# An order table, a head-by-head start and VectorE adds in a fused attention and feed-forward kernel

## The chip, the cores and the metric

The kernel runs on one core of a Trainium2 chip. The metric is device time in microseconds; of the kernel before, three runs were taken: 113.99, 114.84 and 115.63, median 114.84. PE is TensorE, DVE is VectorE, ACT is ScalarE, POOL is GpSimd, SP is SyncE, which only issues transfers here.

## What is computed

Attention with a polynomial sketch (batch 4, 4 heads, 1088 tokens, head size 32, sketch size 8), followed by a feed-forward layer with the activation h - tanh(h):

```python
def phi(x):                                   # S1, S2: 8 x 32
    a = einsum('rd,bhsd->bhsr', S1, x)
    b = einsum('rd,bhsd->bhsr', S2, x)
    return einsum('bhsi,bhsj->bhsij', a, b).reshape(..., 64)
q_p, k_p = phi(q), phi(k)
kv  = einsum('bhsf,bhsd->bhfd', k_p, v)
z   = sum(k_p, axis=2)
num = einsum('bhsf,bhfd->bhsd', q_p, kv)
den = einsum('bhsf,bhf->bhs', q_p, z)[..., None] + 1e-06
x   = (num / den)  as 4352 tokens x 128
h   = x @ w_in                                # 128 x 2048
out = (h - tanh(h)) @ w_out                   # 2048 x 128, float32
```

## The kernel before

**Attention, batch by batch.** k lands with a block of tokens on each partition. `k_transposes` (L583, DVE) makes kT. `k_sketch` (ksk, PE, 64x32 tiles) gives both sketches of k, and two DVE transposes (L616, kab) bring them back as abk. `gram` with `scmm` (PE, two small ACT copies gm and sc between and behind them) prepares the weight that yields the denominator. `k_outer` (L659, DVE) makes the products w, 768 elements a partition, three per batch; `kv_part` (kvmm; sckv with scmm in batches 1 to 3) sums them with v on PE. `kv_tail` copies (kvd), transposes (kvt) and copies again (kvb). For q: a DVE transpose (qT), `q_sketch` (qsk, PE, 32x32 tiles), a transpose back (abc, L729), then on DVE the product m, the sum den, the reciprocal rd, the quotient aq (tile ap), and in `q_piece` products qp of 512 or 768 elements (L767), each transposed (qpT, L772). num (L783, PE, 32x32 tiles) multiplies them with kvb, and x copies on ACT or DVE put the result into xT as bf16. All attention matmuls are float32. Batch 0 is cut into a piece of 2 blocks of 128 tokens (the first 256 columns of xT), one of 3 and one of 4; batch 1 into 5 and 4, the others are one piece of 9.

**Feed-forward.** The 4352 columns of xT are ten groups, `GCOLS = [256, 384, 448] + [512] * 6 + [192]` (g0 to g9). Per group, 16 matmuls h (L877) go into PSUM, ACT applies tanh(-h) to each (L881, th, bf16, 20 buffers; from g7 on in pairs of 1024 columns), and 16 matmuls o (L892) sum th with w_out into one bank. The term h @ w_out is added as a correction: wc = w_in @ w_out is made once on PE, kept as two bf16 parts wch and wcl, and two matmuls c per group (L896) add it. DVE transposes the result (ot, L901) and SP stores it. Ahead of this the weights are cast to bf16 on ACT or POOL (wi, wo), and w_in is transposed on PE and copied by ACT (wiT).

**PSUM.** Eight banks: h of g0 to g6 use banks 0, 1 and 2 in turn, o bank 3, attention banks 4 to 7. From g7 on, h takes pairs of banks (4-5, 6-7, 0-1).

**Order.** Each step is recorded with the tiles it reads and writes. `_Prog.schedule` then simulates the five engines while the program is built: a step has a key, a price (`_v`, `_a`, `_pe` and others) and may have several engines; at each moment the ready step with the lowest key within a window is placed, and a PSUM bank or a buffer is chosen for it. Where PE would be idle it inserts matmuls of zeros (`fill`, L435). `sync` then puts semaphore waits where a step needs one of another engine, or the result of an earlier step of its own engine. Each engine runs its list in order. Loads are issued by SP in an order of keys, with at most 1.4 MB under way.

Of the kernel before, what the change touches and what calls it, by code (L numbers as in the profile page):

```python
# [18 lines left out]
GCOLS = [256, 384, 448] + [512] * 6 + [192]  # L19
T_FIRST = 12500.0  # L20
PERIOD = 8900.0
FILL = (214.0, 60.0)
CAP = 1.4e6
PAIRS = 7
URGENT = (-60500.0, 450.0)
PIECES = {0: [(0, 2), (2, 5), (5, 9)], 1: [(0, 5), (5, 9)], 2: [(0, 9)], 3: [(0, 9)]}
OFF = [[0, 9], [17, 26]]
WINDOW = {"tensor": 60.0, "vector": 150.0, "scalar": 60.0, "gpsimd": 30.0, "sync": 30.0}


class _Bank:
    __slots__ = ("t", "ops")

    def __init__(self):
        self.t, self.ops = 0.0, []
# [51 lines left out]
class _Op:  # L87
    __slots__ = ("engs", "fn", "key", "deps", "users", "nleft", "vals", "eng", "lat", "mode",
                 "t0", "t1", "seq", "known", "waits", "inc", "cnt", "sem", "dma", "name", "filler")


class _Prog:
    SWITCH = 125.0
# [4 lines left out]
    def add(self, engs, fn, r=(), w=(), key=0.0, chain=None, dma=0, name="", after=(), mode=None):  # L98
        o = _Op()
        o.engs = engs  # L100
        o.fn, o.key, o.dma, o.name, o.mode = fn, key, dma, name, mode
        o.deps, o.users, o.vals = {}, [], []
        o.filler = False
# [31 lines left out]
    @staticmethod  # L135
    def pick(grp, t):
        best = None
        for c in grp.pool.choices:
            a = 0.0
            for bank in c[0]:  # L140
                if bank.t is None:
                    break
                a = max(a, bank.t)
            else:
                if a <= t and grp.pool.psum:
                    return t, c
                if best is None or a < best[0]:
                    best = (a, c)
        return best and (max(t, best[0]), best[1])

    def schedule(self, filler=None):
        for o in self.ops:
            o.nleft = len(o.deps)
            for d in o.deps:
                d.users.append(o)
            o.t1 = None
        ready = [o for o in self.ops if o.nleft == 0]
        free = {"tensor": 1100.0, "vector": 900.0, "scalar": 900.0, "gpsimd": 900.0, "sync": 700.0}
        self.order = {e: [] for e in free}
        wire = 0.0  # L160
        pemode = None
        fills = True

        def start_of(o, e):
            t = free[e]
            for d, raw in o.deps.items():
                if d.eng == e and not d.dma and e == "tensor":
                    continue
                if d.eng == e and not d.dma:
                    if raw:  # L170
                        t = max(t, d.t1 + d.lat - 45.0)
                    continue
                t = max(t, d.t1 + (0.0 if d.dma else d.lat))
            for v in o.vals:
                if v.grp is not None and v.grp.ap is None:
                    best = self.pick(v.grp, t)
                    if best is None:
                        return None
                    t = best[0]
            return t  # L180

        n = 0
        while n < len(self.ops):
            best = None
            for e in free:
                cands = []
                for o in ready:
                    if e in o.engs:
                        t = start_of(o, e)
                        if t is not None:  # L190
                            cands.append((t, o))
                if not cands:
                    continue
                t0 = min(t for t, _ in cands)
                t, o = min(((t, o) for t, o in cands if t <= t0 + (URGENT[1] if o.key < URGENT[0] and not o.dma else WINDOW[e])), key=lambda x: (x[1].key, x[0]))
                rank = (t, o.key, o.engs[e][0])
                if best is None or rank < best[0]:
                    best = (rank, t, o, e)
            assert best is not None, "stuck"
            _, t, o, e = best  # L200
            for v in o.vals:
                g = v.grp
                if g is not None:
                    if g.ap is None:
                        _, c = self.pick(g, t)
                        g.ap = c[1]
                        m = len(c[0]) // len(g.vals)
                        for u in g.vals:
                            u.banks = c[0][u.index * m:(u.index + 1) * m]
                            u._ap = c[1][u.index]  # L210
                            u.first_deps = [d for bank in u.banks for d in bank.ops]
                            for bank in u.banks:
                                bank.t = None
                    if o in v.phases[0][2]:
                        for d in v.first_deps:
                            o.deps.setdefault(d, d.eng == e and d.seq == len(self.order[e]) - 1)
            if e == "tensor":
                if o.name == "o0.0":
                    fills = False
                if filler is not None and t - free[e] > 200.0 and fills:  # L220
                    self.fill(filler, free[e], t)
                if pemode is not None and o.mode != pemode:
                    t += self.SWITCH
                pemode = o.mode
            o.eng, o.t0 = e, t
            occ, o.lat = o.engs[e]
            if o.dma:
                free[e] = t + occ
                wire = max(t + 1450.0, wire) + o.dma
                o.t1 = wire + (300.0 if o.key < -79000 else 2000.0)  # L230
            else:
                o.t1 = t + occ
                free[e] = o.t1
            o.seq = len(self.order[e])
            self.order[e].append(o)
            ready.remove(o)
            n += 1
            for v in o.vals:
                v.left -= 1
                if v.left == 0 and v.grp is not None:  # L240
                    last = v.phases[-1][2]
                    for bank in v.banks:
                        bank.ops = list(last)
                        bank.t = max(d.t1 + (0.0 if d.dma else d.lat) for d in last)
            for u in o.users:
                u.nleft -= 1
                if u.nleft == 0:
                    ready.append(u)
        self.end = max(o.t1 for o in self.ops)

    def fill(self, filler, a, b):
        t = a
        while t + FILL[0] + FILL[1] < b:
            o = _Op()
            o.engs = {"tensor": (FILL[0], 215.0)}
            o.fn, o.key, o.dma, o.name, o.mode = filler[0], 0, 0, "fill", "128x128"
            o.deps, o.users, o.vals = {filler[1]: True}, [], []
            o.filler = True
            o.eng, o.t0, o.t1, o.lat = "tensor", t, t + FILL[0], 215.0
            o.inc, o.sem, o.waits, o.known = False, None, [], {}  # L260
            o.seq = len(self.order["tensor"])
            self.order["tensor"].append(o)
            t = o.t1

    def sync(self, nc):
# [4 lines left out]
        while len(done) < total:  # L270
            moved = False
            for e, lst in self.order.items():
                while pos[e] < len(lst) and all(d in done for d in lst[pos[e]].deps):
# [3 lines left out]
                    for d in sorted(o.deps, key=lambda d: -d.t1):  # L277
                        raw = o.deps[d]
# [43 lines left out]
def _v(n):  # L322
    return {"vector": (n / 0.96 + 64.0, 143.0)}


def _vp(n):
    return {"vector": (n / 0.96 + 76.0, 158.0)}


def _a(n):  # L330
    return {"scalar": (n * 0.8333 + 50.0, 175.0)}


def _as(n):
    return {"scalar": (n * 0.8333 + 65.0, 190.0)}


def _g(n, c=1.05):
    return {"gpsimd": (n * c + 130.0, 150.0)}


def _pe(ns):
    return {"tensor": (ns, 215.0)}


def bass_polysketch_attn__then__act_tanh_shrink_kernel(
# [38 lines left out]
    att1 = one(4, 5, 6, 7)  # L385
    att2 = _Pool([(pb[i:i + 2], [bank(i), bank(i + 1)]) for i in (4, 6)], True)
# [3 lines left out]
    kL = [sb("kL", [128, NC * 32]) for _ in range(B)]  # L390
    vL = [sb("vL", [128, H, NB * 32]) for _ in range(B)]
    qL = [sb("qL", [128, NC * 32]) for _ in range(B)]
    kT_p = pool("kT", 2, [128, 36 * 32])
    qTs = [sb("qT", [128, 36 * 32]) for _ in range(B)]
    abk_p = pool("abk", 2, [128, 2, NB, 32])
    abc_p = pool("abc", 2, [128, NB, H, 32])
    w_p = _Pool([([_Bank() for _ in range(3)], [sb("w", [128, 3 * 256]) for _ in range(3)])])
    qp_p = pool("qp", 3, [128, 3 * 256])
    qpT_p = pool("qpT", 2, [128, 9 * 256])
    m_p = pool("m", 2, [128, NB * H, 9])  # L400
# [5 lines left out]
    wqs = [sb("wq", [128, 32]) for _ in range(2)]  # L406
    wqc = [_Val(ap=w[:, 0:16]) for w in wqs]
    kvb_p = pool("kvb", 4, [128, 2, 128])
    NTH = 20
# [581 lines left out]
```

## Time and profile before

| | |
|---|---|
| three runs | 113.99, 114.84, 115.63 us |
| profiled execution, first to last instruction | 112.6 us |
| bytes read and written | 8.81 MB and 2.23 MB |
| first h, first tanh | 19.71 us, 20.03 us |
| last o ends, last ot starts | 108.87 us, 108.89 us |
| tanh on ACT (L881) | 136 instructions, 69.5 us |
| products of 768 on DVE (w, qp) | 0.98, 0.94 us mean |
| work of POOL after 20 us | none |

The profiled execution's own time is its span; what a run takes above it lies before the first and behind the last instruction, 2.2 us by the median. Idle columns in the profile say how long an engine stood still before an instruction and what released it. Durations of matmuls overlap: two that follow each other start closer together than either lasts.

### The profile page before, as it was taken

To read this page: it belongs to the slowest core of one execution; us is meant where nothing else is said; L and a number is where in the kernel's file an instruction comes from. 1 tells how busy PE (TensorE), PEld (TensorE's weight loads), DVE (VectorE), ACT (ScalarE), POOL (GpSimd) and SP (SyncE) were. 2 spreads that over 40 slices of the span, in tenths; PEclk is the share of its full clock that TensorE was granted. 3 is DMA by queue.
4 is the path that set the end of the run, shared out by engine and by line. 5 is a ranking of instruction groups with operands and counts; after the bars stand their busy time and mean duration, and the time that the engine had idled before them with its cause. 6 is when DMAs were issued, how large, how long until landed. Compare 5 with 4: busy or idle time off the path is not lost.

```text
span 112.6 us, 3409 instructions
## 1 busy us (share of the span) xinstructions
PE 100.3 (89%) x1467; PEld 48.7 (43%) x1477; DVE 72.1 (64%) x115; ACT 79.9 (71%) x164; POOL 5.6 (5%) x25
## 2 busy tenths in 40 slices
PE   6975996998799989979999999979999999999960
PEld 4523783455355444436443346334243334334540
DVE  4469374899999999999999992499950020020030
ACT  2101247876487798586599867798969999999950
POOL 5202016000000000000000000000000000000000
PEclk9999999999999999999999999999999999999999
DMA  1999878799987804022000230005004106005035
GB/s 21 259 245 329 255 232 234 243 241 272 226 270 218 165 5 69 0 47 46 0 6 0 44 49 6 6 11 83 0 6 68 25 0 93 0 12 77 4 55 73
DMA packets 25037, 11.24 MB, mean 100 GB/s; under 512 B 18880, under 2 KB 23616, under 8 KB 25024
## 3 DMA queue, kind: packets, MB, share of 16 engines
q1 hardware_dynamic: 24320, 10.97, 40.7%
q8 instruction: 11, 0.18, 0.7%
q10 hardware_dynamic: 704, 0.08, 0.5%
q14 instruction: 2, 0.02, 0.1%
HBM read 8.81 MB, written 2.23 MB: 98 GB/s over the span
## 4 chain that ended last, share of the span: by engine, by line
PE 36%; ACT 28%; DVE 16%; DMA 13%; issue 2%; SPq 1%; DVEq 0%
ACT th L881 25%; PE psb L892 11%; PE psb L877 10%; DMA qL<-in_q_dram 5%; DMA wo_f<-in_moe_w_out_dram 5%; PE psb L783 5%; DVE qp L767 4%; DVE qpT L772 4%; DVE abc L729 3%; DMA kL<-in_k_dram 3%; PE psb L724 3%; PE psb L671 3%; DVE ot L901 2%; PE psb L610 2%; ACT wiT L375 2%
## 5 line engine op out<-in xcount | busy, mean ns | idle before, releaser
L881 ACT ACTIVATE th<-psb 128x512 bf16<-128x512 f32 (+4 forms) x136 | 69.5, 624 | 7.4 <-PE psb L877 6.6
L877 PE MATMUL psb<-xT,wi 128*128 128x512 bf16 (+4 forms) x155 | 50.1, 349 | 1.5 <-DVE xT L375 0.5
L892 PE MATMUL psb<-th,wo 128*128 128x512 bf16 (+4 forms) x157 | 48.2, 348 | 1.4 <-DVE ot L901 0.6
L877 PEld LDWEIGHTS psb<-xT,wi 128*128 128x128 bf16 x160 | 14.9, 97 | 25.3 <-ACT th L881 14.4
L892 PEld LDWEIGHTS psb<-th,wo 128*128 128x128 bf16 x160 | 14.6, 97 | 15.7 <-ACT th L881 7.5
L901 DVE STREAM_TRANSPOSE ot<-psb 128x512 f32<-128x512 f32 (+4 forms) x10 | 6.3, 626 | 22.6 <-PE psb L892 22.6
L772 DVE STREAM_TRANSPOSE qpT<-qp 128x768 f32<-128x768 f32 (+1 forms) x14 | 12.1, 861 | 0.4
L767 DVE TENSOR_TENSOR qp<-ap,abc 128x768 f32<-128x768 f32 (+1 forms) x14 | 11.5, 818 | 0.1
L659 DVE TENSOR_TENSOR w<-abk 128x768 f32<-128x768 f32 x12 | 11.3, 981 | 0.1
L729 DVE STREAM_TRANSPOSE abc<-psb 128x1152 f32<-128x1152 f32 (+2 forms) x5 | 5.7, 1143 | 5.1 <-PE psb L724 5.0
L435 PE MATMUL psb<-zz 128*128 128x256 bf16 x33 | 7.8, 388 | 1.1 <-DVE zz L434 1.1
L783 PE MATMUL psb<-qpT,kvb 32*32 32x128 f32 (+4 forms) x448 | 8.3, 309 | 0.1
L375 ACT CAST xT<-psb 128x192 bf16<-128x192 f32 (+4 forms) x8 | 3.3, 421 | 5.4 <-PE psb L783 5.4
L583 DVE STREAM_TRANSPOSE kT<-kL 128x576 f32<-128x576 f32 (+1 forms) x8 | 5.6, 724 | 1.7 <-DMA kL<-in_k_dram 1.7
L783 PEld LDWEIGHTS psb<-qpT,kvb 32*32 32x32 f32 x448 | 5.1, 103 | 2.9 <-DVE qpT L772 2.0
L671 PE MATMUL psb<-w,vL 128*32 128x64 f32 x288 | 6.0, 243 | 0.0
L592 DVE STREAM_TRANSPOSE qT<-qL 128x1088 f32<-128x1088 f32 (+2 forms) x5 | 5.3, 1055 | 0.9 <-DMA qL<-in_q_dram 0.9
L435 PEld LDWEIGHTS psb<-zz 128*128 128x128 bf16 x33 | 4.1, 135 | 3.6 <-DVE zz L434 1.1
L671 PEld LDWEIGHTS psb<-w,vL 128*32 128x32 f32 x288 | 5.1, 125 | 0.3 <-issue 0.2
L642 ACT COPY gm<-psb 128x32 f32<-128x32 f32 x4 | 0.8, 198 | 5.6 <-PE psb L638 5.6
L724 PE MATMUL psb<-qT,wq 32*32 32x288 f32 (+2 forms) x160 | 3.6, 381 | 0.9 <-ACT xT L375 0.9
L375 DVE CAST xT<-psb 128x192 bf16<-128x192 f32 (+3 forms) x6 | 2.8, 467 | 1.1 <-PE psb L783 1.0
(55 smaller groups left out, 56.6 us busy)
## 6 DMA issues: line engine op xcount, KB each, us to landing
kL<-in_k_dram SPq DMA_DIRECT2D x3, 544.0 KB, 3.6
qL<-in_q_dram SPq DMA_DIRECT2D x3, 544.0 KB, 4.9
vL<-in_v_dram SPq DMA_DIRECT2D x4, 288.0 KB, 4.8
vL<-in_v_dram SPq DMA_DIRECT2D x4, 256.0 KB, 5.0
wi_f<-in_moe_w_in_dram SPq DMA_DIRECT2D x4, 256.0 KB, 4.7
wo_f<-in_moe_w_out_dram SPq DMA_DIRECT2D x4, 256.0 KB, 5.8
out_dram<-ot SPq DMA_DIRECT2D x16, 64.0 KB, 2.0
out_dram<-ot SPq DMA_DIRECT2D x8, 56.0 KB, 1.9
```

Of the source, the lines that this page charges most:

```text
L375: return e.copy(o, i) if name == "scalar" else e.tensor_copy(o, i)
L435: filler = (lambda e, n: e.matmul(bank(3)[:, 0:256], zz.ap[:, 0:128], zz.ap[:, 128:384], start=True, stop=True), zop)
L659: P.add(_v(768), lambda e, n: e.tensor_tensor(out=wv.ap.rearrange("p (x i j) -> p x i j", i=8, j=8), in0=abh(0)[:, :, :, None].to_broadcas ...
L671: i = e.matmul(pv[b].ap[h * 32:(h + 1) * 32, 0:64], vL[b][:, h, blk * 32:(blk + 1) * 32], wvs[b, p].ap[:, (bi * 4 + h) * 64:(bi * 4 + h + ...
L729: P.add(_vp(sn * 4), lambda e, n: e.transpose(abc.ap.rearrange("p k h f -> p h k f")[:, :, 0:s1 - s0, :], psa4[:, :, 0:sn].rearrange("p h ...
L767: P.add(_v(cn * 256), lambda e, n, qp=qp, c0=c0, cn=cn: e.tensor_tensor(out=qp.ap[:, 0:cn * 256].rearrange("p (x i j) -> p x i j", i=8, j= ...
L772: P.add(_v(cn * 256), lambda e, n, qp=qp, o0=o0, cn=cn: e.transpose(qt.ap[:, o0 * 256:(o0 + cn) * 256], qp.ap[:, 0:cn * 256]), r=[qp], w=[ ...
L783: i = e.matmul(psa4[h * 32:(h + 1) * 32, g, 0:nb * 32], kvb.ap[g * 32:(g + 1) * 32, x, h * 32:(h + 1) * 32], qq[g * 32:(g + 1) * 32, 0:nb, ...
L877: P.add(_pe(n_ / 2.4 + 2.6), lambda e, n, jb=jb, hv=hv: e.matmul(hv.ap[:, jb % m * 512:jb % m * 512 + n_], wi[jb // 4].ap[:, (jb % 4) * 12 ...
L881: P.add(_a(n_ * m), lambda e, n, hv=hv, th=th: e.activation(out=th.ap.rearrange("p (u x) -> p u x", u=m)[:, :, 0:n_], in_=hv.ap.rearrange( ...
L892: fn = lambda e, n, x=x, st=st, sp_=sp_: e.matmul(ov.ap[:, 0:n_], wo[x // 4].ap[:, x % 4, :], ths[x][0].ap[:, ths[x][1] * 512:ths[x][1] * ...
L901: P.add(_vp(n_), lambda e, n: e.transpose(ot.ap[:, 0:n_], ov.ap[:, 0:n_]), r=[ov], w=[ot], key=-60000, name=f"ot{gi}")
```

## The change

**Order.** The scheduler is gone, with its keys, windows and prices. `TABLE`, a text of 861 entries, lists every step by number, its engine (v, a, g, t, s) and the bank or buffer that it takes; `f` and `F` are fills of 256 and of 512 columns. `plan` reads it. `sync` now also waits for every earlier step of the same engine that a step depends on, PE excepted. A step that is marked `lock` on DVE waits for the last locked step on POOL ahead of it in the table, and the other way round; products of two SBUF tiles are locked, and POOL's casts.

**POOL.** w, m, aq and qp may go to POOL. By the table all qp do, 7 of the 12 w, and most m; of the two-input products DVE keeps five w and most aq.

**Batch 0.** The first group has 384 columns, the next two 352 each (`GCOLS = [384, 352, 352] + ...`). The first 384 tokens get a path of their own, `q_heads`: a block-diagonal weight wqd (four heads at once) makes the sketch one 128x128 matmul of 384 columns, `kv_heads` makes a block-diagonal kvd0 (kvh, kve), and products and num go in two halves of 192 columns, 128x128 tiles. The rest of batch 0 is one piece of 6 blocks. k's sketch is cut into even and odd blocks.

**VectorE.** `GDIR = {5: 192, 6: 320, 7: 320, 8: 320}`: for so many columns of these groups, 1152 in all, DVE adds h to tanh(-h) (dg), so that o holds the whole activation there and c is left to the other columns.

**Other.** scmm of batches 1 to 3 is one matmul, followed by two small DVE steps (scx, sc); k is loaded in two halves by column, v in four parts, each q in two; S2 is loaded by SP; batch 3 uses the buffers of k and q of batch 0; th has 18 buffers of its own, and 16 more in the float32 weights' place once these are cast.

```diff
-GCOLS = [256, 384, 448] + [512] * 6 + [192]
+GCOLS = [384, 352, 352] + [512] * 6 + [192]
-CAP = 1.4e6
+CAP = 1.45e6
+GDIR = {5: 192, 6: 320, 7: 320, 8: 320}
+CUT0 = [0, 12, 34]
-PIECES = {0: [(0, 2), (2, 5), (5, 9)], 1: [(0, 5), (5, 9)], 2: [(0, 9)], 3: [(0, 9)]}
+PIECES = {0: [(3, 9)], 1: [(0, 5), (5, 9)], 2: [(0, 9)], 3: [(0, 9)]}
+TABLE = """
+0v 10g 16s 15a 8g 11g 18s 7g 1g 17s 2g 19s 4v 21s 22s 29s 62v:0 30s 63v 20s 5v 64v 50v 23s 51v F F F F F F F F F F
...
+    def plan(self, table, filler):
...
+            if o.lock and e in lastl:
+                d = lastl["gpsimd" if e == "vector" else "vector"]
+                if d is not None:
+                    o.deps.setdefault(d, False)
+                lastl[e] = o
...
-                            if d.eng == e and not (raw and e != "tensor"):
+                            if d.eng == e == "tensor":
                                 if not o.dma:
                                     continue
...
+    def kv_heads():
+        P.add(_vp(64), lambda e, n: e.transpose(kvh.ap, pv[0].ap[:, 0:64]), r=[pv[0]], w=[kvh], name="kvh")
+        P.add({**_v(256), **_gt(256)}, lambda e, n: e.tensor_tensor(
+            out=kvd0.ap.rearrange("p x (h v) -> p x h v", h=H),
+            in0=kvh.ap.rearrange("p (x v) -> p x v", x=2)[:, :, None, :].to_broadcast([128, 2, H, 32]),
+            in1=maskh.ap[:, None, :, None].to_broadcast([128, 2, H, 32]), op=ALU.mult),
+            r=[kvh, maskh], w=[kvd0], name="kve", lock=True)
+
+    def q_heads(i):
...
+        P.add(_pe(70 + nx * 53.3, 230.0), lambda e, n: e.matmul(
+            pq.ap[:, 0:nx * 32], wqd.rearrange("p h f -> p (h f)"), qt_.ap, start=True, stop=True),
+            r=[qt_, wqds, wqdc], w=[pq], mode="128x128", name=f"qsk0.{i}")
...
+            def num(e, n, qt=qt, pn=pn, a=a, z=z):
+                qq = qt.ap[:, 0:(z - a) * 64].rearrange("p (c x t) -> p c x t", x=2, t=32)
+                for x in range(2):
+                    r = e.matmul(pn.ap[:, 0:(z - a) * 32], kvd0.ap[:, x, :], qq[:, :, x, :], start=(x == 0), stop=(x == 1))
+                return r
...
-            P.add(_v(cn * 256), lambda e, n, qp=qp, c0=c0, cn=cn: e.tensor_tensor(
+            P.add({**_v(cn * 256), **_gt(cn * 256)}, lambda e, n, qp=qp, c0=c0, cn=cn: e.tensor_tensor(
...
+                if gc:
+                    P.add(_vp(gc * m), lambda e, n, hv=hv, th=th: e.tensor_tensor(
+                        out=th.ap.rearrange("p (u x) -> p u x", u=m)[:, :, 0:gc],
+                        in0=hv.ap.rearrange("p (u x) -> p u x", u=m)[:, :, 0:gc],
+                        in1=th.ap.rearrange("p (u x) -> p u x", u=m)[:, :, 0:gc], op=ALU.add),
+                        r=[hv, th], w=[th], name=f"dg{gi}.{jb // m}", lock=True, after=[act])
...
-                    ov.ap[:, 0:n_], x.ap[:, :], xt, start=st, stop=sp_)
+                    ov.ap[:, gc:n_], x.ap[:, :], xt[:, gc:n_], start=st, stop=sp_, skip_group_check=bool(gc))
```

More of the change, by code (lines that the diff above doesn't have):

```diff
@@ L151, in schedule @@
[L151 to L203, printed above, removed]
@@ L871, in ffn @@
         m = 2 if late else 1
+        gc = GDIR.get(gi, 0)
         ths = []
```

705 lines of the change are left out of this document (379 added, 326 removed).

## The prediction

> **What bounds the kernel now.** I read the chain of waits first, then the stages, then single rows. The page:
>
> ```profile
> span 112.6 us, 3409 instructions
> PE 100.3 (89%) x1467; PEld 48.7 (43%) x1477; DVE 72.1 (64%) x115; ACT 79.9 (71%) x164; POOL 5.6 (5%) x25
> ```
>
> PE leads, but its busy time overlaps itself. The chain shows how the feed-forward part began, and what a matmul costs:
>
> ```profile
> 10.71 5.61 DMA wo_f<-in_moe_w_out_dram
> ...
> 16.34 0.62 ACT wo L375
> 16.96 1.83 ACT wiT L375 x2
> 18.79 0.18 ACT xT L375
> 18.96 0.14 issue
> 19.10 0.81 PE psb L724 x32
> ...
> 65.04 0.22 PE psb L877
> 65.25 0.22 PE psb L892
> 65.47 0.22 PE psb L877
> 65.68 0.21 PE psb L896
> 65.90 1.53 PE psb L783 x63
> 67.43 0.16 issue
> 67.59 0.38 PE psb L896
> ```
>
> The last x of the first group stood behind ACT's wo and wiT copies, although its product had ended about 17.8; the first h starts at 19.71. In the run at 65 us, 512-column matmuls start 0.216 apart, and a return from small tiles adds about 0.16.
>
> So I count PE's work from the first h to the last o (19.71 to 108.87, 89.2 us). FFN columns: 16 x 4352 for h, as many for o, 2 x 4352 for c: 147,968 x 0.216/512 = 62.4. Attention, from the chain's pieces: num 0.96, 1.07, 1.06, 1.02, 1.53, 1.53; per batch 1 to 3 ksk 0.68, gram 0.20, sckv 1.20, kvt 0.26, qsk 0.84; wc 0.9: together 17.6. Rest: 9.2, of which 34 changes of tile size x 0.155 = 5.3, so 3.9 idle. PE is the bound; ACT is not:
>
> ```profile
> 19.70:28.75 9.05, 8.60 (x191) 4.75 (x182) 8.54 (x15) 6.28 (x21) 0.00 (x0) 1.00 0.87 246
> 28.75:72.40 43.65, 40.78 (x764) 19.45 (x771) 38.59 (x57) 33.58 (x77) 0.00 (x0) 1.00 0.32 72
> 72.40:108.90 36.50, 35.36 (x233) 14.58 (x235) 12.79 (x18) 34.19 (x56) 0.00 (x0) 1.00 0.20 31
> ```
>
> Columns after the length: PE, PEld, DVE, ACT, POOL. ACT idles 15 us here, DVE is near full to 72 and nearly free after, POOL has nothing.
>
> **Work removed from PE.** c is skipped for 1152 columns: 2 x 1152 x 0.42 ns = 0.97 us. Batch 0 keeps one num of 6 blocks (between 1.07 for 4 and 1.53 for 9: 1.25) for two (2.03): 0.78. scmm is one matmul for four, in batches 1 to 3 (0.18 to about 0.07): 0.33. New total after the first h: 61.4 + 16.5 = 77.9. Tile changes there are 32 for 34.
>
> **The head.** Bytes lead: the new order has 2.785 MB up to the last wi and 3.05 to wo0. Before, 1.507 MB had landed by 9.70 (wi0) and 3.24 by 17.17, 0.23 MB per us; so wi3 lands near 15.1, wo0 near 16.3, batch 1's k (3.60) near 18.7. Walk, record lengths from rows, 0.05 a hop: the two k halves carry the bytes they did; the smaller transposes (288 columns 0.47), S2 queued behind k on SP, and q's 384 columns (0.57, landing near 7.3) in front of kab end kab at 8.75 instead of 8.13. w0.0 and w0.1 0.95 each, wqs to 10.9. Then POOL makes w0.2. No 768 product on POOL is in the trace; the nearest rows are s2r (two inputs, 128 elements, 0.40) and casts of 128 and 512 (0.29, 0.61). If it grew like a cast it takes 0.83, if the whole of s2r above a memset's 0.10 is per element 1.9; with a cast's fixed 0.18, 1.5. I take 1.6, to 12.55; the ends move all that follows by -0.8 or +0.3. kvmm0.2 and kvh to 13.35, rd, aq to 13.85, POOL's qph0.0 0.85, kve 0.6, qph0.1 0.85 to 16.2 with num0.0 beside them; qpTh 0.57, num0.1 0.8 (f32, 2 x 192 columns: 0.57 by three of kvt's 128-column transposes of 0.19, 0.9 by ksk's 288 columns in 0.68; qsk0 the same), x 0.32: first h near 18.0. ACT meanwhile has kvd0 after kvh at 13.4, then wi, wi, kvb, wi, wi, wiT, wo, wiT: 5.5 us by the starts of such rows, so the first tanh is near 19.0, against 20.03. That is the later one: h0.2 needs wiT1's bank. From there 16 tanh of 384 columns start 0.38 apart (6.1), and wo1, gm, wch, three copies stand among them (2.3): th0.15 ends at 27.4, its h at 27.0. PE has by then 7.0 us of work behind it (16 h, 9 o, ksk1, gram1, wc, num0.3); before, at 27.0, about 5.8. POOL's casts and products of batch 1 fit in it, barely (wo3, w1.0, w1.2 end near 26.2, kvmm1 can start at 27.3).
>
> By the Trainium skill, GPSIMD Engine Reference, section 3.1 Elementwise, a two-input elementwise operation on GpSimd takes about 2.6 cycles an element; that makes 768 elements an estimated 1.7 us plus dispatch, and the first tanh some 0.2 later than in the walk and the sum 110.4. The same page, section 4.1 Engine selection, leaves such work on VectorE, which speaks against this change; no run here shows the 768 form.
>
> **Products and their semaphores.** DVE products and POOL work do collide:
>
> ```profile
> L659 DVE TENSOR_TENSOR w<-abk x3: 950/959/1361, 8.2 to 9.9; 128x768 f32<-128x768 f32 x3
> ```
>
> The third w began at 9.90 under a POOL cast of 9.70 to 10.46 and took 0.41 longer; a DVE transpose beside casts (qT, 832 columns, 16.74) took 1.00, as its length has it. The lock keeps products apart, and puts a wait in DVE's queue: behind scx1 stand wcl, sc1, w1.1, kT2, so a late POOL product delays them, then kvmm1 and qsk1. In return DVE sheds all 14 qp (8 x 0.94 + 6 x 0.66 = 11.5 us) and 7 of the 12 w (0.95 each). Chain from qsk1 to num1.0: abc 1.38, qT and ot 1.8 beside m, scx to aq 1.75, POOL 1.6 + 1.1, qpT 0.7: 8.4, against 8.7 of PE's work and tile changes that the new order puts between them. So it costs 0 while a 768 product stays under about 1.9, and 1 us a batch for each 0.6 above.
>
> The Trainium skill, SBUF — State Buffer, section Who interferes with whom, says that the later of a two-input VectorE operation and a reading GpSimd one blocks until the first ends. That would have made the third w 0.56 longer where the row has 0.41; the sum has neither, as the order forbids the overlap.
>
> **The added DVE work.** PSUM rows: wcl 128 columns 0.25, xT 320 0.49, 512 0.69, abc 896 1.12; so dg of 192, 320, 640 columns takes 0.32, 0.49, 0.82: 5.1 + 7.8 + 13.1 = 26 us, in the stretch where DVE idles 23.7 of 36.5 and less of attention is left to it. It holds a bank longer: a pair needs h 0.6, tanh 1.03, dg 0.82 and hops 0.15 = 2.6 for three pairs, 0.87 each, against PE's 0.86; a single in group 6 1.65/3 = 0.55 against 0.43 and its share of attention. I take 0; the ends are 0 and 16 x 0.05 + 16 x 0.08 = 2.1, and no gain, as nothing starts earlier by it. SP issues four v loads a batch for two (0.63 each, +1.3): hidden, as only stores wait behind them; uncovered, a k would land 1.3 late. DVE's instructions wait 168 times for 119, POOL's 21 for 11; a wait already met shows as a step of 0.02 between DVE rows: 1 us of DVE's 30 idle ones.
>
> **Sum.** 27.0 + (77.9 - 7.0) + 27 changes x 0.155 (4.2) + idle as before past 28.75 (80.1 spent, 73 worked, 31 x 0.155: 2.2) = 104.3 for the last o; the tail of ot and stores as before, 3.7: span 108.0. The median stands 2.2 over the profiled span (114.84 to 112.6): 110.2.
>
> **Rivals.** (B) The head gives nothing: wi, k or wo land 2 us later than the straight line says and ACT's eight copies go with them. Then the work alone (2.1) and little else remains: 112.6. For it, wi1 landed 1.3 off the line; against it, wi3 and wo0, on which ACT hangs here, landed within 0.4 (14.5 and 16.3 for 14.9 and 16.1). (C) Slower: POOL products are the new chain. At 2.6 us a 768 product (+1.0) the head moves by about 2, and each batch's chain (w, two to three qp in line) outruns its PE cover by some 1.5 to 2, three times: 110.2 + 2 + 5.5 = 117.7. It decides from about 2.4; s2r's row puts 1.9 as its upper end, DVE's queue speaks for it as scx and w wait there in order. (D) Earlier still: a fixed order with 34 th buffers for 20 lets h run ahead, the 2.2 of idle and the 0.9 lost to the first group go, and num and POOL are at their low ends: 106.5. That the order is not what it says can't be: it is read from a list.
>
> **Numbers.** Forecast 110.2 (its own range 107.5 to 112.5) 0.62; B 0.15; C 0.10; D 0.13. The range leaves out the outer part of D and C: 106.2 to 113.8. Two per cent, 2.3 us, is about what these runs can tell (113.99 to 115.63): under 112.5 lie the forecast, D and a little of B, 0.77; above 117.1 most of C, 0.08; between, 0.15.
>
> **What would show it.** First tanh near 19.0 with ACT's nine copies just before it; POOL products of 768 at 1.5 to 1.9 and DVE products at 0.95 throughout; idle PE before kvmm1 and num1 under 1 us; the last o near 104.3; c of groups 5 to 8 shorter. A POOL product over 2.4, DVE waiting on POOL for more than some 5 us in all, or PE waiting for dg would make the forecast wrong.

## The result, and the profile after

The changed kernel takes 104.98 us (median; 104.74 to 105.40), the kernel before 114.41 (113.99 to 115.63) in the same session: a ratio of 0.917, 95% interval 0.912 to 0.923. That is 9.4 us, where 4.6 were forecast, and 1.2 us below the range. Some executions of a kernel are slower as a whole; the ratios leave these out, and so do the times of the runs below. The profiled execution:

```profile
span 102.9 us, 3160 instructions
PE 95.5 (93%) x1309; PEld 48.2 (47%) x1318; DVE 78.2 (76%) x143; ACT 81.5 (79%) x163; POOL 36.5 (35%) x54
```

POOL went from 5.6 to 36.5 us of work; DVE has 6 us more in all: it lost its products and got 26 us of adds. PE is still the engine that is nearest to full. The chain of waits, at its start:

```profile
6.33 0.58 DVE qT L572
6.91 0.74 DVE abk L591 x2
7.67 1.30 DVE w L643 x2
8.97 0.44 issue
...
9.68 1.52 POOL w L643
...
12.51 1.04 ACT wi L359 x2
...
13.82 1.04 ACT wi L359 x2
14.87 0.91 ACT wiT L359
15.78 0.52 ACT wo L359
16.29 0.91 ACT wiT L359
17.22 0.50 ACT th L921
```

The chain is the one that was walked, with ACT's copies just ahead of the first tanh, but each link is earlier: q landed at 6.33 (7.3 forecast), the abk transposes end at 7.65 (8.75), the first tanh starts at 17.22 (19.0) and the first h at 16.85 (18.0). The windows from the first h to batch 1's kv, from there to batch 2's num, and on to the last o (columns: length, then busy time of PE, PEld, DVE, ACT and POOL):

```profile
16.85:25.40 8.55, 8.38 (x143) 4.29 (x142) 5.49 (x10) 7.34 (x19) 7.43 (x10) 1.00 0.94 280
25.40:55.70 30.30, 29.88 (x557) 16.31 (x561) 25.37 (x41) 28.58 (x71) 17.48 (x16) 1.00 0.41 108
55.70:98.95 43.25, 42.55 (x397) 20.30 (x401) 35.15 (x63) 39.24 (x65) 4.46 (x3) 1.00 0.22 33
```

PE is busy in 98% of every stretch, where it had 93 to 97% before. ACT, which idled 15 us after the first h, is now at 91% behind 55.7. What PE's own waits list shows is shortest to read beside that of before (engine, line, releaser; us in total, times, longest). Before:

```profile
PE psb L724 <- ACT xT L375: 0.9, 1, 0.9
PE psb L610 <- ACT th L881: 0.7, 1, 0.7
PE psb L599 <- DVE kT L583: 0.7, 1, 0.7
PE psb L892 <- DVE ot L901: 0.6, 1, 0.6
PE psb L877 <- DVE xT L375: 0.5, 1, 0.5
```

After, past its first 10 us:

```profile
PE psb L917 <- issue: 0.5, 3, 0.2
PE psb L938 <- ACT th L921: 0.2, 1, 0.2
PE psb L917 <- ACT wi_f L921: 0.2, 1, 0.2
PE psb L938 <- DVE th L926: 0.2, 1, 0.2
```

The rows on batch 1's kT, on a bank behind a tanh and on an xT copy are gone, and no wait after the first h is longer than 0.2 us. (th tiles in the place of the cast weights are listed as wi_f and wo_f. The row of L917 on issue is no wait: at its three places, 50.76, 57.46 and 77.47, the trace has the weight load of one more matmul and no record of the matmul itself.)

**Where the time went.** PE's time from the start of the first h to that of the last o, split by the starts of its matmuls: the feed-forward matmuls at 0.216 us for 512 columns; the attention runs, which are the stretches between two feed-forward matmuls that hold other work, with the waits in them; and what is left, idle inside feed-forward runs. The trace lacks the records of ten of the 340 feed-forward matmuls before and of nine after, while their weight loads (PEld) are all there. The table puts these matmuls where their loads show them; without that, those next to an attention run would be counted as part of it (22.8 and 19.8 us instead of 21.5 and 18.8).

| us | before | after | change | forecast |
|---|---|---|---|---|
| first h starts | 19.71 | 16.85 | -2.9 | -1.7 |
| feed-forward matmuls | 62.4 | 61.5 | -1.0 | -1.0 |
| attention runs | 21.5 | 18.8 | -2.7 | -1.4 |
| idle in feed-forward runs | 5.0 | 1.5 | -3.5 | about -0.5 |

The removed c came off as forecast. The other three rows fell by more than forecast, by 1.2, 1.3 and 3.0 us, and most of that is not work. The tail behind the last o is 0.2 longer.

### The profile page after: what moved, and what is told of

Its sections match the earlier page's. It is cut to its first block, busy times and chain, and to the rows that moved or that the text cites. A ratio compares the mean times of both kernels' runs of the same rounds, so it can differ in the third digit from the quotient of the medians.

```text
span 102.9 us, 3160 instructions
## 1 busy us (share of the span) xinstructions
PE 95.5 (93%) x1309; PEld 48.2 (47%) x1318; DVE 78.2 (76%) x143; ACT 81.5 (79%) x163; POOL 36.5 (35%) x54
## 4 chain that ended last, share of the span: by engine, by line
PE 67%; ACT 12%; DVE 8%; DMA 4%; issue 3%; POOL 1%; SPq 1%; DVEq 0%
PE psb L938 25%; PE psb L917 25%; PE psb L813 5%; ACT th L921 4%; DMA qL<-in_q_dram 4%; ACT wi_f L921 2%; PE psb L942 2%; PE psb L658 2%; PE psb L580 2%; PE psb L754 2%; ACT wi L359 2%; ACT wiT L359 2%; DVE ot L947 2%; POOL w L643 1%; SPq L465 1%
## 5 line engine op out<-in xcount | busy, mean ns | idle before, releaser
L917 PE MATMUL psb<-xT,wi 128*128 128x512 bf16 (+3 forms) x154 | 46.5, 347 | 0.7 <-issue 0.5
L921 ACT ACTIVATE th<-psb 128x512 bf16<-128x512 f32 (+3 forms) x77 | 41.0, 592 | 3.7 <-PE psb L917 2.2
L938 PE MATMUL psb<-th,wo 128*128 128x512 bf16 (+3 forms) x89 | 25.4, 343 | 0.4 <-ACT th L921 0.2
L917 PEld LDWEIGHTS psb<-xT,wi 128*128 128x128 bf16 x160 | 14.9, 97 | 21.0 <-DVE th L926 3.0
L797 POOL TENSOR_TENSOR qp<-ap,abc 128x768 f32<-128x768 f32 (+1 forms) x12 | 16.6, 1405 | 7.5 <-DVE ap L779 7.4
L921 ACT ACTIVATE wi_f<-psb 128x512 bf16<-128x512 f32 (+3 forms) x31 | 16.7, 621 | 0.7 <-PE psb L917 0.6
L921 ACT ACTIVATE wo_f<-psb 128x512 bf16<-128x512 f32 (+2 forms) x28 | 16.5, 621 | 0.4 <-PE psb L917 0.2
L926 DVE TENSOR_TENSOR th<-psb,th 128x320 bf16<-128x320 f32 (+2 forms) x24 | 13.5, 566 | 2.1 <-ACT th L921 1.2
L643 POOL TENSOR_TENSOR w<-abk 128x768 f32<-128x768 f32 x7 | 10.6, 1518 | 6.9 <-DVE abk L591 4.4
L938 PE MATMUL psb<-wi_f,wo 128*128 128x512 bf16 (+2 forms) x36 | 10.2, 343 | 0.1
L938 PE MATMUL psb<-wo_f,wo 128*128 128x512 bf16 (+1 forms) x32 | 10.2, 362 | 0.0
L813 PE MATMUL psb<-qpT,kvb 32*32 32x288 f32 (+3 forms) x320 | 6.7, 348 | 0.0
```

What stands on the lines that cost most here:

```text
L643: P.add({**_v(768), **_gt(768)}, lambda e, n: e.tensor_tensor(out=wv.ap.rearrange("p (x i j) -> p x i j", i=8, j=8), in0=abh(0)[:, :, :, N ...
L797: P.add({**_v(cn * 256), **_gt(cn * 256)}, lambda e, n, qp=qp, c0=c0, cn=cn: e.tensor_tensor(out=qp.ap[:, 0:cn * 256].rearrange("p (x i j) ...
L813: i = e.matmul(psa4[h * 32:(h + 1) * 32, g, 0:nb * 32], kvb.ap[g * 32:(g + 1) * 32, x, h * 32:(h + 1) * 32], qq[g * 32:(g + 1) * 32, 0:nb, ...
L917: P.add(_mm(n_), lambda e, n, jb=jb, hv=hv: e.matmul(hv.ap[:, jb % m * 512:jb % m * 512 + n_], wi[jb // 4].ap[:, (jb % 4) * 128:(jb % 4 + ...
L921: act = P.add(_a(n_ * m), lambda e, n, hv=hv, th=th: e.activation(out=th.ap.rearrange("p (u x) -> p u x", u=m)[:, :, 0:n_], in_=hv.ap.rear ...
L926: P.add(_vp(gc * m), lambda e, n, hv=hv, th=th: e.tensor_tensor(out=th.ap.rearrange("p (u x) -> p u x", u=m)[:, :, 0:gc], in0=hv.ap.rearra ...
```

## The experiments

Theory 1 is that DVE's queue was what PE waited for, that POOL's products relieved it, and that the semaphores keep the two from slowing each other. The rivals: that the added adds gain (or cost) time; that the head is worth less than it shows; that the order, above all the longer lead of h over o, makes the gain. The lead is the number of tiles of h issued on PE whose o isn't yet issued: in front of an o, in the order of PE's weight loads, it is 1 to 9 before, mostly 3 to 8, and 8 to 21 in groups 2 to 7 of the changed kernel, 19 at batch 2's num. (The expectations below put it at 1 to 5 and at 11 to 13, which is too narrow.) All comparisons are with the kernel before, 114.0 to 114.4 in each session.

**a_qp_dve.** The ten qp of batches 1 to 3 go back to DVE, in the same places of the table:

```diff
-149g:1
+149v:1
...
-228g:1
+228v:1
```

> The changed kernel with the ten products qp of batches 1 to 3 on DVE instead of POOL, every step at its place in the table, all else as it is. Theory 1 (relief of DVE): PE's idle time went because DVE no longer makes these products and attention runs ahead of the feed-forward part; then this returns most of the 4 to 5 us of idle: 108 to 110 us. Theory 2 (order alone: h placed far ahead of o): DVE has room for 8.7 us more, and it stays within 1 us of the changed kernel's 105.0: 104.5 to 106.

108.81 us, ratio 0.954 (0.948 to 0.960): 3.8 us are given back. Attention runs 21.9 (18.8 in the changed kernel), idle in feed-forward runs 3.4 (1.5). PE's waits name the transposed products, which now queue on DVE:

```profile
PE psb L813 <- DVE qpT L802: 1.5, 1, 1.5
PE psb L917 <- DVE th L926: 1.4, 1, 1.4
```

L813 is num; the second row is a bank that an add, queued behind the products, holds. Theory 1 held.

**a_w_dve.** The same with six w of batches 1 to 3 (`133g:3` becomes `133v:3`, and so on).

> The changed kernel with the six products w of batches 1 to 3 that POOL makes on DVE, at their places in the table; qp stay on POOL. Theory 1 (DVE's relief is what counts): 5.7 us more for DVE against 8.7 with the ten qp, so 1 to 2.5 us slower, 106 to 107.5. If only the chain behind qsk counts, in which w has no part: 104.8 to 105.4.

106.51 us, 0.934 (0.928 to 0.939): 1.5 us given back. Held.

**a_all_dve.** Both edits together.

> The changed kernel with all ten qp and all six w of batches 1 to 3 on VectorE. Alone, qp cost 3.8 and w 1.5 us. Theory 1 (VectorE's queue is the clock of attention, each product in it counts): the sum or more, 109.8 to 111.5 us. Theory 2 (the order hides most, both shared one cover): under 109.5.

110.09 us, 0.966 (0.963 to 0.969): 5.1 us, the sum of the two (5.3) within their spread. Attention runs 22.3, idle in feed-forward runs 3.5. POOL's products of batches 1 to 3 are worth some 5 us in this order. With them on DVE the changed kernel still takes 3.9 us less than the one before, and 2.5 of it is the head (first h at 17.21 for 19.71).

**b_pool.** The other way round: the kernel before, its scheduler free to put w and qp on POOL, no semaphores between products.

```diff
+def _gt(n):
+    return {"gpsimd": (n * 1.8 + 120.0, 175.0)}
...
-        P.add(_v(768), lambda e, n: e.tensor_tensor(
+        P.add({**_v(768), **_gt(768)}, lambda e, n: e.tensor_tensor(
...
-            P.add(_v(cn * 256), lambda e, n, qp=qp, c0=c0, cn=cn: e.tensor_tensor(
+            P.add({**_v(cn * 256), **_gt(cn * 256)}, lambda e, n, qp=qp, c0=c0, cn=cn: e.tensor_tensor(
```

> The kernel before with POOL allowed for the products qp and w, by its own scheduler, which puts 9 of 14 qp and 5 of 12 w there; no lock, nothing else changed. Theory 1: x comes earlier and PE's idle time shrinks: faster by 3 us or more, below 111.5. Theory 2: the lead of h stays at 4 to 6 tiles and little is gained: 113 to 115. Collisions of products on DVE and POOL may eat up to 2 us of a gain.

116.24 us, 1.019 (1.011 to 1.027), past what either theory had. The products w (shortest, median and longest in ns):

```profile
L663 DVE TENSOR_TENSOR w<-abk x7: 957/959/2270, 7.7 to 58.6; 128x768 f32<-128x768 f32 x7
L663 POOL TENSOR_TENSOR w<-abk x5: 1507/2285/2287, 7.7 to 57.8; 128x768 f32<-128x768 f32 x5
```

A w of DVE takes 0.96 us or, in three of seven cases, 2.27: those that start while POOL has one under way. One of POOL takes 1.51 alone and, in four of five cases, 2.28, behind one of DVE. The second stands until the first is done, so side by side the two engines gain little. POOL alone isn't the gain.

**b_lag and b_pool_lag.** A lead for the scheduler: the key of every o set later, so that up to 12 tiles of h go ahead, in the kernel before and in b_pool.

```diff
-key=t0 + i * step + 1500
+key=t0 + i * step + 5000
```

> The kernel before with one number changed: the key of each o is 5000 behind its group's start instead of 1500, so that its scheduler places h up to 12 tiles ahead of o (5 before). Theory 2 (order alone): PE's idle time goes as in the changed kernel, 3 to 4 us: 110.5 to 112. Theory 1 (relief of DVE): x arrives no earlier, the lead falls to 0 at num1.0 all the same: within 1.2 us of before, 113.2 to 115.

> Both edits on the kernel before: POOL for products and the key of o 5000 behind. Theory 1: as with POOL alone, at most 1 us better. Theory 2: as with the later o alone. If each needs the other, the pair gains more than both together: 108.5 to 110, and PE's rest beyond work falls from 9 to about 5 us.

113.20 us, 0.993 (0.988 to 0.998), and 116.73, 1.022 (1.012 to 1.032). The lead alone brings about 1 us to the kernel before, nothing to b_pool; the gain that was expected of the pair did not come. (At batch 1's num the lead of b_lag was 0 all the same: there was no x to work on.)

**b_pool_lock and b_pool_lock_lag.** b_pool with products kept apart, in the scheduler's simulation and by a semaphore wait; then with the later key too.

```diff
+            if o.lock and lastl[other[e]] is not None:
+                t = max(t, lastl[other[e]].t1 + lastl[other[e]].lat)
...
+            if o.lock:
+                if lastl[other[e]] is not None:
+                    o.deps.setdefault(lastl[other[e]], False)
+                lastl[e] = o
```

> The kernel before with POOL allowed for qp and w, and with products on DVE and POOL kept apart by its scheduler and by a semaphore. If collisions of products were what made POOL alone slower (two w on DVE in 3.15 us, one beside them on POOL in 2.29): below 113, and no DVE product of 768 above 1.1 us. If the scheduler's order is the limit whatever POOL takes: 113.5 to 116.

> As the last, with the key of each o 5000 behind its group's start, which places h about 10 tiles ahead of o. If relief of DVE and a lead of h are both needed, and enough: 109 to 111.5, 1.5 us or more better than the lock alone. If the table's order holds more than these two: 112 or above.

123.14 us, 1.076 (1.072 to 1.081), and 113.97, 0.999 (0.994 to 1.003). The products hardly disturb each other now (DVE's w 1037 ns in the mean, POOL's 1516), yet the first is much slower, past both of its expectations. PE's longest wait in it:

```profile
PE psb L796 <- DVE abc L742: 6.6, 2, 6.0
```

L796 is num. The scheduler took all sketches of q first and reached batch 1's num only at 58.4 us (46.5 before). With the lead the loss goes, and from the first h on PE then needs 87.3 us (before 88.9, after 81.9): attention runs fell to 19.8, but 5.1 of idle in feed-forward runs is as much as before, and the head and the tail take 0.6 more each. Theory 1 as it stood, relief and semaphores, fell here as a sufficient cause: it needs an order that uses the freed queue.

**a_no_lock.** The table without the waits between products:

```diff
-            if o.lock and e in lastl:
+            if False and o.lock and e in lastl:
```

> The changed kernel without the semaphores that keep the products of DVE and POOL apart; order and engines the same. If the lock matters because overlapping products delay each other: slower by 1 us or more, with DVE products of 768 above 1.2 us and POOL ones above 1.7. If the table already has them apart in time: same within 0.5 us. If the lock's waits cost time: faster by 0.5 to 1.

105.89 us, 0.928 (0.922 to 0.933): 0.9 us slower, all of it in the head (first h at 17.81 for 16.85; from there on 81.9 in both). The timeline of DVE, then of POOL, in the kernel without waits:

```profile
7.40 3.14 DVE L643 TENSOR_TENSOR w<-abk 128x768 f32<-128x768 f32 x2
10.47 0.18 DVE L632 TENSOR_TENSOR wqd<-psb,maskh 128x32 f32<-128x32 f32 x1
```

```profile
7.45 2.28 POOL L643 TENSOR_TENSOR w<-abk 128x768 f32<-128x768 f32 x1
```

The first line holds two products of different length (shortest, median and longest in ns):

```profile
L643 DVE TENSOR_TENSOR w<-abk x2: 959/1613/2267, 7.4 to 8.3; 128x768 f32<-128x768 f32 x2
```

And in the changed kernel, DVE and then POOL:

```profile
7.67 1.83 DVE L643 TENSOR_TENSOR w<-abk 128x768 f32<-128x768 f32 x2
9.41 0.18 DVE L632 TENSOR_TENSOR wqd<-psb,maskh 128x32 f32<-128x32 f32 x1
```

```profile
9.68 1.51 POOL L643 TENSOR_TENSOR w<-abk 128x768 f32<-128x768 f32 x1 [2.30 <-DVE wqd L632]
```

Two products of DVE and one of POOL take 3.14 us side by side and 1.83 + 1.51 = 3.34 one after the other. Side by side each stands behind the one under way: DVE's first takes 0.96, POOL's, started 0.05 later, 2.28 to 9.73, and DVE's second, started at 8.3, 2.27 to 10.54. So the semaphore saves hardly any time; it decides who is first. DVE's are, and wqd, on which q's sketch hangs, comes at 9.41 and not at 10.47. POOL's third w then ends at 11.19, when the sketch has just been transposed (abc, to 11.18).

**a_late.** Two more ACT copies of 512 columns ahead of the first tanh, into a tile that nobody reads:

```diff
+    late = sbv("late", [128, 512], BF16)
+    for z in range(2):
+        one_more = P.add(_a(512), lambda e, n, z=z: copy(e, n, late.ap, wiT[0] ...[:, z * 512:(z + 1) * 512]), ...)
```

> The changed kernel with two more ACT copies of 512 columns in front of the first tanh, about 1.05 us. If PE's work from the first group on is the bound, the head counts one to one: 105.9 to 106.3. Rival: the first group has slack or ACT's later slack takes it in: under 0.4 us more, 104.8 to 105.4.

106.12 us, 0.929 (0.924 to 0.935), 1.1 us slower. In the profiled execution the first tanh comes at 17.96 (0.7 later), and it took 105.58 for 104.74, 0.8 more. A shift of the head counts about one to one, so the 2.8 us by which the first tanh came earlier (17.22 for 20.03) stand in the sum nearly whole.

**a_no_dg and a_dg78.** The table without VectorE's adds, c again over all columns; then with the adds of groups 7 and 8 only.

```diff
-GDIR = {5: 192, 6: 320, 7: 320, 8: 320}
+GDIR = {}                      # a_no_dg
+GDIR = {7: 320, 8: 320}        # a_dg78
```

> The changed kernel without VectorE's additions of h (no dg, c over all columns); order otherwise the same. If PE's work is the bound to the end: slower by the 0.97 us of c that comes back, 105.7 to 106.3. Rival: dg holds h's banks longer and costs PE as much as c did; then no difference, 104.6 to 105.4.

> The changed kernel with VectorE's additions of h in groups 7 and 8 alone, where h has three pairs of banks; groups 5 and 6, where h has three single banks, do c over all columns again. Theory (the gain of dg is eaten by waits for banks, above all for the single ones): 0.53 us of c stay saved and few waits are left: 0.3 to 0.5 us under the 105.0 of the changed kernel and of that without dg. Rival (pairs wait as much): 104.9 to 105.2.

104.97 us (104.69 to 105.14), ratio 0.920 (0.914 to 0.925), and 105.23 (104.31 to 105.82), 0.919 (0.914 to 0.924): no difference from 104.98. (The runs of a_dg78 lie 1.5 us apart; the 0.3 to 0.5 that its theory named can't be told from them.) The 26 us of adds are worth nothing here. The profiled executions show where c's 1.0 went. Without the adds the attention runs are as long (18.8 and 18.8), idle in feed-forward runs is 1.2 instead of 1.5, and the last o ends at 99.49 instead of 98.94. The half microsecond that is left is lost behind it: from the last o to the end of the span it is 3.4 us without the adds and 4.0 with them. a_no_lock and a_late, with the adds, have 4.0 too; why the end takes longer is open.

**b_dg.** The adds alone, in the kernel before (no c for the 1152 columns, VectorE adds h there instead):

> The kernel before with VectorE's additions of h alone (192, 320, 320, 320 columns of groups 5 to 8, c shortened); its scheduler places them. If PE's work bounds the end there as well: faster by about 1.0 us, 113.2 to 113.9. If DVE, which still makes the products up to 72 us, delays them: no gain or slower by 1 to 2 us.

129.66 us, 1.136 (1.128 to 1.145). The longest waits:

```profile
ACT xT L376 <- PE psb L784: 15.3, 6, 10.7
...
PE psb L784 <- DVE qpT L773: 8.3, 1, 8.3
```

L784 is num of batch 3. Its transposed products queue on DVE behind the adds, PE stands 8.3 us (the granted clock from 60 to 100 us is 0.91), and ACT's copy of x waits 10.7 with everything behind it. The loss is many times the 1 to 2 us expected. In the kernel before there was no room on DVE for adds ahead of batch 3; in the changed kernel POOL has made it. The run says what an order without regard for DVE would do; it isn't the price of the adds.

**a_short5 and a_short8.** The table re-dealt: every place of a feed-forward matmul on PE and every attention step stays, but h is held back so that at most 5 (8) tiles of it are ahead. tanh and adds move with their h, ot with its last o:

```diff
-315a:19 316t:1 167v 296t 103s 318t:0 141a:1 320t:2 173g:1 317a:20 143t:0 ...
+315a:19 296t 167v 297t 103s 298t 141a:1 299t 173g:1 143t:0 101s 300t ...
```

(296 to 300 are o of group 0; 316, 318 and 320 are h of group 1, 315 and 317 its tanh.)

> The changed kernel with its feed-forward matmuls re-dealt: the places of h and o on PE and every attention step keep their place in the order, but at most 5 tiles of h are issued ahead of their o (11 to 13 in the changed kernel, 1 to 5 before). tanh, VectorE's adds and the transposes of outputs move with their matmuls. Theory 1 (the gain is VectorE's relief by POOL, the lead is not needed): 104.5 to 105.6 us. Theory 2 (a long lead is what hides late x and late ACT copies, and carries most of the 3.4 us of idle that went from the feed-forward runs): 107 to 108.5 us, with the excess inside feed-forward runs back at 4 to 6.

> The changed kernel with at most 8 tiles of h ahead of their o instead of 5. Theory A (the loop of h, tanh and add has to fit in the lead: 2.6 us over 4 pairs is 0.65, under PE's 0.87): most of the loss goes, 105 to 109 us. Theory B (every tile of lead counts alike, between 5 and about 12): about 114 to 116 us.

123.84 us, 1.087 (1.083 to 1.090), and 119.17, 1.042 (1.035 to 1.049). Both are far past every expectation: the changed kernel with a lead of 5 is slower than the kernel before. From 94 us on, in the groups of pairs, a_short5 shows the loop. DVE's adds, then PE's o that waits for them:

```profile
99.21 0.82 DVE L926 TENSOR_TENSOR wi_f<-psb,wi_f 128x640 bf16<-128x640 f32 x1 [0.51 <-ACT wi_f L921]
100.46 0.83 DVE L926 TENSOR_TENSOR wi_f<-psb,wi_f 128x640 bf16<-128x640 f32 x1 [0.42 <-ACT wi_f L921]
101.79 0.82 DVE L926 TENSOR_TENSOR wi_f<-psb,wi_f 128x640 bf16<-128x640 f32 x1 [0.51 <-ACT wi_f L921]
```

```profile
101.34 0.39 PE L938 MATMUL psb<-wi_f,wo 128*128 128x512 bf16 x1 [0.21 <-DVE wi_f L926]
101.57 0.81 PE L917 MATMUL psb<-xT,wi 128*128 128x512 bf16 x2
102.67 0.39 PE L938 MATMUL psb<-wi_f,wo 128*128 128x512 bf16 x1 [0.29 <-DVE wi_f L926]
```

A pair every 1.25 to 1.33 us, where PE has 0.87 of work for it: tanh waits for h, the add for tanh, o for the add, and h is held behind o. a_short8 shows no such waits in its paired stretch, as its expectation has it; nearly all its loss lies before that, up to group 6, where o waits for ot, num and q's sketch for ACT's kvb, h for a bank behind a tanh. Its theory A, that the loop of h, tanh and add was all of the cost, fell.

One more run, a_all_dve_short5, had both edits: a lead of 5, and the ten qp and six w on DVE. It was expected at 111.5 to 114 us, or as a_all_dve if the lead mattered nowhere, and took 125.16, 1.098 (1.092 to 1.103). So at a lead of 5 POOL's products are worth 1.3 us (125.16 for 123.84), where they are worth 5.1 in the table's own order.

**a_short5_no_dg.** a_short5 without the adds.

> The kernel with at most 5 tiles of h ahead, without VectorE's adds (c covers all columns). In the kernel with 5 tiles ahead, a pair of h, its tanh (1.02 us) and its add (0.82) follow one another at 1.25 to 1.33 us a pair where PE's work is 0.87, and past 80 us the feed-forward runs hold some 11 us of excess. Theory A (the add lengthens a loop that a lead of 5 tiles, two and a half pairs, can't cover; without it the loop is about 1.8 us for 2.5 pairs): those 11 go and c's 1 us comes back, 112 to 115 us. Theory B (the short lead by itself is what costs): over 120 us.

115.39 us, 1.012 (1.008 to 1.017): 8.4 us back, and just past theory A's range. So the adds cost 8 us at a lead of 5 tiles and nothing at the changed kernel's. The remaining 10 us have another cause: in these three kernels the tanh also stand differently among ACT's copies, so what they lost isn't the lead alone.

**a_o_early.** The cleanest of the four: the kernel without adds, with h, tanh, copies and attention steps in the order they had, and only every o from group 2 on five places earlier:

```diff
-363t:0 365t:1 339a:28 172v ...
+363t:0 346t 365t:1 347t 339a:28 172v ...
```

(363 and 365 are h of group 2, 346 and 347 are o of group 1.)

> The kernel without VectorE's adds (105.0 us) with every o from group 2 on five places earlier, so that 5 to 15 tiles of h are ahead for 10 to 19, and h, tanh, the copies and the attention steps in the order they had. Theory 1 (the lead by itself is worth little, the pattern of h, copies and attention is what keeps PE fed): 104.8 to 106 us. Theory 2 (each tile of lead counts, as 19 us for 7 tiles would have it): over 110 us.

110.84 us, 0.973 (0.969 to 0.977), 5.9 us slower than a_no_dg. That is past theory 2's bound, though not at its rate for each tile. The attention runs are the same (18.7 and 18.8), the idle in feed-forward runs is 7.1 instead of 1.2. It lies in two places. One is where a group's first o follows the last o of the group before. PE and then DVE at such a place:

```profile
69.66 0.38 PE L936 MATMUL psb<-th,wo 128*128 128x512 bf16 x1
69.87 0.38 PE L915 MATMUL psb<-xT,wi 128*128 128x512 bf16 x1
70.84 0.39 PE L936 MATMUL psb<-th,wo 128*128 128x512 bf16 x1 [0.59 <-DVE ot L945]
```

```profile
70.07 0.72 DVE L945 STREAM_TRANSPOSE ot<-psb 128x512 f32<-128x512 f32 x1 [4.83 <-PE psb L936]
```

Up to group 6 o has one bank, and ot must empty it (0.72 and the hops): one h stands between, which fills 0.2 of it. Five such places take 0.5 to 0.8 each, 3.5 us. The other is the end, where the lead has run out and each o waits for its tanh: 2.7 us past 99.

## Why the prediction was wrong

The direction, the chain and most prices held; the size was off by a factor of two. Of the 5.2 us between forecast and result, 1.2 lie in the head and 4.2 between the first h and the last o (86.3 forecast, 82.1 measured); the tail took 0.2 back. The step that failed is what the sum adds to PE's work: "27 changes x 0.155 (4.2) + idle as before past 28.75 (80.1 spent, 73 worked, 31 x 0.155: 2.2)", and the 2.0 of the same kinds ahead of 27.0. These are 8.4 us in all; the trace after has about 4.1.

- **The price of a change of tile size.** "A return from small tiles adds about 0.16" was read from one place, the issue of 0.16 at 67.43 behind num, and given to 34 changes. There is no such price at that place. PE's load of the weights of one more h stands there, and only the record of its matmul is missing:

```profile
67.36 0.10 PEld L877 LDWEIGHTS psb<-xT,wi 128*128 128x128 bf16 x1 [0.47 <-issue]
```

 The gap of 0.16 is that h. a_no_lock, whose trace has all 340 feed-forward matmuls, shows the same place (num of 9 blocks, then h) without a gap:

```profile
56.80 1.53 PE psb L813 x63
58.33 0.54 PE psb L917 x2
```

 The price put attention's work and changes at 17.6 + 5.3 = 22.9 us before; the trace has 21.5, and that with waits in it: batch 1's ksk run took 1.51 us before and 0.86 after, one gram run 0.81 against 0.40. After, the same bookkeeping gave 16.5 + 32 x 0.155 = 21.5, and 18.8 was measured. That is 2.3 beyond the counted work, 0.07 a change. So some 3 us of waiting before were taken for a fixed price that no order could end.
- **The idle.** It was carried over whole, because no part of the change was named that would end it. Its causes were in the waits list of before: batch 1's kT, an xT copy, a bank, an ot. Of the 5.0 us of idle in feed-forward runs 3.5 went. With POOL's products back on DVE it is 3.4 (a_qp_dve) and 3.5 (a_all_dve) for 1.5; o five places earlier bring 5.9 of it (a_o_early). So two things made it go, and neither does it alone: DVE's queue was relieved (5.1 us by a_all_dve, in idle and attention runs), and the order puts work between a wait's cause and PE's need. Relief under the scheduler's order gave nothing in the whole (b_pool, b_pool_lock_lag), and little at a lead of 5 (1.3, a_all_dve_short5); the order without relief 3.9 us, 2.5 of it the head.
- **The head.** Every link was right and the walk 1.2 us late at the first h, 1.8 at the first tanh: q landed 1 us earlier than the byte line had it, so abk ended 1.1 earlier. a_late shows that this counts nearly one to one.
- **POOL's product.** Taken at 1.6 us, bounds 0.83 to 1.9: measured 1.51 to 1.52. The groups, by shape:

```profile
L797 POOL TENSOR_TENSOR qp<-ap,abc 128x768 f32<-128x768 f32 x9 | 13.5, 1515 | 7.5 <-DVE ap L779 7.4
L643 POOL TENSOR_TENSOR w<-abk 128x768 f32<-128x768 f32 x7 | 10.6, 1518 | 6.9 <-DVE abk L591 4.4 <-DVE wqd L632 2.3 <-DVE scx L622 0.3
L643 DVE TENSOR_TENSOR w<-abk 128x768 f32<-128x768 f32 x5 | 4.7, 952 | 0.1
```

 DVE's stayed at 952, as "0.95 throughout" had it, and rival C's 2.4 was far. By the Trainium skill, GPSIMD Engine Reference, section 3.1 Elementwise, the estimate was 1.7; the trace is 0.2 below. Its section 4.1, Engine selection, leaves such work on VectorE; a_all_dve shows that here this costs 5 us, as VectorE's queue was what PE waited for.
- **The semaphores at 0.** Right for the steady part; in the head they gain 0.9, which wasn't seen. That products on both engines collide was read from the third w and is shown by a_no_lock and b_pool: the one that starts first keeps its length (0.96), the one that starts second stands behind it (2.28 for 1.51, 2.27 for 0.95). The Trainium skill, SBUF — State Buffer, section Who interferes with whom, has the later of such a pair blocked until the first ends; the traces of a_no_lock and b_pool agree.
- **The adds at 0, and c at -0.97.** c gave its 1.0 on PE, and together the two gave nothing. On PE the adds cost about 0.4 in idle, inside the bounds given (0 to 2.1); the other part was lost where the sum had only "as before", in the tail (3.7 forecast, 4.0 with the adds, 3.4 without). The bound was worked out for a loop that has enough tiles ahead. a_short5 shows the condition: at 5 tiles the same adds cost 8 us.
- **Removed attention work.** scmm and batch 0's one num fewer are in the -2.7 of attention runs and weren't separated.
- **The rivals.** D was the nearest at 106.5, by the right effect (idle 2.2 goes) and partly the wrong reason: the table never has more than 20 th tiles alive, and the kernel before had 20 buffers for them. Its lead would have fitted into these. B and C fell.

What stays open: how much of the order's part is the lead, and how much the place of each copy and transpose; what the m and the batch 0 products on POOL are worth, which stayed there in a_all_dve; and the longer tail. a_o_early prices five places of lead at 5.9 us, at two kinds of place; the re-dealt kernels lost more, with tanh moved too. No version tried is measurably faster than the changed kernel.

## What to carry to other kernels

Don't carry idle over as a constant: name the wait behind each stretch of it, and ask of each whether the change ends it; and when a unit price explains a residue, look at the single places, since waits hide in it. Before a gap is called a price, check that nothing ran in it: compare the number of matmul records with that of weight loads. Work that moves to an idle engine pays only with an order that lets the freed queue run ahead, and an order with a long lead only with a queue that can follow: price the two together. A loop through several engines (h, tanh, add, o) costs nothing while enough tiles are ahead of it; work out from the loop's length how many that is before a step is added to it.

## What the runs showed of the hardware

Of two-input products of 768 float32 elements on VectorE and GpSimd, the one that starts second stands until the first is done. In a_no_lock and b_pool such a product takes 0.96 us on VectorE and 1.51 on GpSimd where nothing is in its way, 2.27 and 2.28 where the other engine was first; so two and one take 3.14 us together, where 3.34 is their sum apart. A mean over both kinds (1520 ns on VectorE in b_pool) is the length of none. A transpose on VectorE kept its length beside GpSimd's product: qT of 704 columns took 0.90 us under the w of 9.68 to 11.19, on the line from 0.58 for 384 columns to 0.96 for 768. GpSimd's product grows nearly in a line: 851 ns for 384 elements, 1075 for 512, 1515 for 768, so about 1.7 ns an element and 0.2 us besides. A trace can lack single matmul records, here up to ten of 340, while the weight loads are complete; such a hole behind an attention run is listed as an issue gap of 0.16 us.
